# An attention and mixture-layer kernel: products with V, row shifts, warm-up and weight conversion placed elsewhere in the slots

## The chip, the cores and the metric

The kernel runs on one core of a Trainium2 chip. The metric is device time in microseconds (us), from the launch to the end of one execution. The core has TensorE (PE: matrix products, written to PSUM), VectorE (DVE), ScalarE (ACT), GpSimd (POOL) and DMA queues, of which SyncE (SP) starts most. PSUM has eight banks; a tile of `[128, 2, 512]` float32 takes two of them. PE, DVE, ACT and POOL each run their own list of instructions in order and wait for each other by semaphores.

## The reference, cut to what matters

```
q_rot, k_rot = rotate(q), rotate(k)             # rotary positions; 4 batches, 8 heads, 576 positions, 64 wide
scores = (q_rot @ k_rot.T) / 8
attn = exp(scores - max(scores)); attn = attn / (sum(attn) + 1e-9)
x = (attn @ v), heads side by side              # 2304 x 512
h = x @ w_in                                    # 2304 x 2048
out = (max(h, 0) + log1p(exp(-abs(h)))) @ w_out # 2304 x 512
```

All of it is float32. The kernel keeps that precision by splitting an operand into a high and a low part (`float32r`) and adding three products: high by high, low by high, high by low.

## The kernel before

**Attention in slots.** The 32 heads are taken as 16 pairs; the two heads of a pair lie on partitions 0 to 63 and 64 to 127, so that matmuls come in twos that run side by side ("a pair of matmuls" below), each over 288 columns. A pair of heads has ten slots. The loop at line 565 runs over slots s from 0 to 171; r is s modulo 10 and p is s divided by 10. Three stages are interleaved on PE in each slot:

- `p1(s)` (line 394) computes scores with queries on the partitions, three pairs of matmuls into a PSUM tile called s1, of which there is only one. VectorE reduces it to the negated row maximum (`mx`, line 408). After slots with r = 5 and r = 9, `shift0` (line 417) gathers the maxima of five or ten blocks (`sf`); one slot later `shift1` splits them on GpSimd into a high and a low part (`sh`).
- `shift2` (line 429) transposes these shifts on PE, with six matmuls of 64 columns for the first three blocks of a pair of heads and four for the last two; `shift3` (line 438) copies them from PSUM to `sm` on ScalarE. Before, both stand inside `p1` at r = 7 and r = 1: the transposes go into the free columns of the s1 tile behind the scores, ahead of the reduction in the code, and the copy stands behind it.
- `p2(n2)` with n2 = s - 9 (line 443), the score pass, computes the scores again with keys on the partitions: three pairs of matmuls, and a fourth that adds the shift. It goes to one of two PSUM tiles called s2. `exps` (line 455) exponentiates twice on ScalarE (first to `ph`, the high part, then in place), and `low` (line 462) subtracts on VectorE to give the low part `pl`. A tile s2 is free for the score pass two slots later when `low` has read it.
- `pv_mm(n3, part)` with n3 = s - 12 (line 471) multiplies with V. Five slots make one window, and c3 is n3 modulo 5, so c3 = 0 at r = 2 and 7, and c3 = 4 at r = 1 and 6. A window has 27 pairs of matmuls. In the kernel before, the slots with c3 = 0 to 3 do six of them (three in each of two parts) and the one with c3 = 4 does three. `evac` copies the result out on ScalarE at c3 = 4.

Within a slot PE's order is: part 0 of `pv_mm`, `p2`, part 1 of `pv_mm`, `p1`. Where c3 = 0 it is `p2`, part 0, `p1`, part 1; where c3 = 4 there is no part 1. All is held in the order of the code by `pin`.

**Keys.** The last block of 64 keys is stored twice (`pad`, line 337), so that the weights of the fifth block are 128 columns. ScalarE does this for the first two pairs of heads, GpSimd for the others, two small instructions a pair.

**Weight conversion beside it.** The weights arrive as 64-bit words. For six half-blocks `conv_w(..., spread=True)` (line 104) is advanced once in each slot of the table `PLAN` (line 44): a ScalarE step, a second one, four steps of two VectorE instructions each (`bits` and `sign`, lines 136 and 140), a GpSimd addition, a ScalarE rounding, a GpSimd subtraction. The VectorE steps use free columns of the s2 tile that `low` has just read, so that tile comes free only after them. `LOADS` names the slots in which their DMAs start on SP.

**Rows of x.** From slot 146 on GpSimd also prepares x for the next stage (`split`). GpSimd computes the rotary positions of later pairs throughout.

**Mixture layer.** From line 704 on, `emit_h` and `emit_o` run 96 units of TensorE work. Other conversions stand in it. The change doesn't touch it.

**Ahead of slot 0**, 108 matmuls on zeros (line 311) keep PE occupied while the first loads arrive. In slots 0 to 8 only `p1` runs.

Of the kernel before, what the change touches and what calls it, by code (L numbers as in the profile page):

```python
# [21 lines left out]
SP = 640  # L22
# [21 lines left out]
PLAN = tuple(tuple(b + i for i in (0, 5, 6, 10, 11, 15, 16, 20, 21)) for b in (59, 69, 84, 99, 114, 129))  # L44
LOADS = {33: (0, 0), 38: (0, 1), 43: (0, 2), 48: (0, 3), 53: (1, 0), 58: (1, 1), 63: (1, 2), 68: (1, 3), 73: (2, 0),
         78: (2, 1), 83: (2, 2), 88: (2, 3), 93: (3, 0), 98: (3, 1), 133: (3, 2), 138: (3, 3), 148: (4, 0), 153: (4, 1)}
# [7 lines left out]
def rope_attention_softplus_moe(  # L54
# [231 lines left out]
    def attention(es, es_r, es_s, tail):  # L286
# [3 lines left out]
        hl_p = pool(es, "hl", 3, "right")  # L290
        rp1 = pool(es_r, "rp1", 1, "right")
# [41 lines left out]
        def new_hl(p, i):  # L333
            hl_t[p, i] = hl_p.tile([128, 2, (S, SP)[i]], F32R, tag=f"hl{i}", name=f"hl{i}")
            return hl_t[p, i]

        def pad(t, j, e):
            rnd(t[:, j, S:], t[:, j, 512:S].bitcast(F32), e)

        def rope_steps(p, e="P"):  # L340
            for i in (1, 0):
                r, t = raw_t[p, i], new_hl(p, i)
                a, b = r[:, 1], r[:, 0]
                yield tt(a, a, tab[:, 0, :], ALU.mult, "P")
                yield tt(b, b, tab[:, 1, :], ALU.mult, "P")
                yield tt(a, a, b, ALU.add, "P")
                rnd(t[:, 0, :S], a, e)
                if i:
                    pad(t, 0, e)
                yield  # L350
                tt(t[:, 1, :S], a, t[:, 0, :S].bitcast(F32), ALU.subtract, "P")
                if i:
                    pad(t, 1, e)
                yield
# [4 lines left out]
        def rope_first():  # L359
# [16 lines left out]
            for j in range(2):  # L376
                pad(hl_t[0, 1], j, "A")
# [16 lines left out]
        def p1(n):  # L394
# [12 lines left out]
            x = shift2(s_g[r](p), sp) if r in s_g and s_g[r](p)[0] >= 0 else None  # L407
            pin(nc.vector.tensor_reduce(out=mx[p % 2][:m, j, c, :], in_=sp[:m, :, :HS], axis=AX.X, op=ALU.max,  # L408
                                        negate=True))
            if x is not None:  # L410
                shift3(s_g[r](p), x)
# [15 lines left out]
        s_g = {7: lambda p: (p, 0), 1: lambda p: (p - 1, 1)}  # L427

        def shift2(pg, t):
            p, g = pg  # L430
# [7 lines left out]
        def shift3(pg, x):  # L438
            p, g = pg
            pin(nc.scalar.copy(out=sm[p % 2][:, cut(g), :].rearrange("p c (t x) -> p t c x", t=2),  # L440
                               in_=x.rearrange("p t (c x) -> p t c x", x=64)))

        def p2(n):
            p, r = divmod(n, 10)
            j, c = divmod(r, 5)
            q, k = hl_t[p, 0], hl_t[p, 1]
            ck, cq = slice(c * 128, c * 128 + 128), slice(j * HS, (j + 1) * HS)
            sp = ps2[n] = ps_2.tile([128, 2, 512], F32, tag="s2", name="sp2")
            bias = sm[p % 2].rearrange("p c x -> p (c x)")
            for t, (a, b) in enumerate((*terms, (2, 2))):  # L450
                for i, o in enumerate(rows):
                    lhs, rhs = (k[o, b, ck], q[o, a, cq]) if t < 3 else (ones[o, :], bias[o, cq])
                    pin(nc.tensor.matmul(out=sp[:, i, :HS], lhsT=lhs, rhs=rhs, start=(t == 0), stop=(t == 3)))  # L453

        def exps(n):
            sp = ps2[n][:, :, :HS]
            ph = p_p.tile([128, 2, HS], F32R, tag="ph", name="ph")
            pin(nc.scalar.activation(out=ph, in_=sp, func=AF.Exp, scale=D ** -0.5))  # L458
            pin(nc.scalar.activation(out=sp, in_=sp, func=AF.Exp, scale=D ** -0.5))  # L459
# [9 lines left out]
        side = {}  # L469

        def pv_mm(n, part):
            p, r = divmod(n, 10)
            j, c = divmod(r, 5)
            flip = (c + part) % 2
            if c == 0 and part == 0:
                if n // 5 == NSLOT // 5 - 2:
                    pv_t[n // 5] = ps_1.tile([128, 2, 512], F32, tag="s1", name="pv")
                else:
                    pv_t[n // 5] = ps_v.tile([128, 2, 512], F32, tag="pv", name="pv")
            pv, vt = pv_t[n // 5], vs[p % 2]  # L480
            ph, pl = p_t[n]
            if side.get("flip", flip) != flip:
                hold = pin(nc.tensor.nop())
                for x in side["two"]:
                    tc.add_manual_dep(hold.ins, x.ins.name,
                                      mybir.DependencyInfo(mybir.DependencyClass.Sync, mybir.DependencyReason.DATA))
            two = []
            for t, (w, x) in enumerate(((0, ph), (2, ph), (0, pl))):
                for o in rows:
                    i = (o.start // 64 + flip) % 2  # L490
                    m = 64 if w else 128
                    lhs = vt[o, i, c, w:w + 1 + (w == 0), :].rearrange("p a d -> p (a d)")
                    ins = pin(nc.tensor.matmul(out=pv[:m, i, :HS], lhsT=lhs, rhs=x[o, i, :],  # L493
                                               start=(c == 0 and part == 0 and t == 0),
                                               stop=(t == 2 and c == 4)))
                    if t == 2:
                        two.append(ins)
            side.update(flip=flip, two=two)
            if part or c == 4:
                p_t.pop(n)  # L500
# [53 lines left out]
        nc.gpsimd.memset(ones.bitcast(F32), 1.0)  # L554
        for i in range(2):
# [9 lines left out]
        for s in range(NSLOT + LAG + PVD):  # L565
# [3 lines left out]
            c3 = n3 % 5  # L569
            if has3 and c3:  # L570
# [3 lines left out]
            if has2:  # L574
                p2(n2)
                exps(n2)
# [8 lines left out]
            if s == NSLOT + 1:  # L585
                last = (NP - 1, 1)
                shift3(last, shift2(last, ps_1.tile([128, 2, 512], F32, tag="s1", name="st")))
# [184 lines left out]
```

## Time and profile before

| | us |
|---|---|
| median of 3 runs | 737.51 |
| the three runs | 737.23 to 738.17 |
| the profiled execution | 738.13 |
| its span, first to last instruction | 736.3 |
| PE busy | 709.4 (96%) |
| DVE busy | 483.0 (66%) |
| ACT busy | 390.2 (53%) |
| POOL busy | 312.4 (42%) |

Busy time of PE is a union of records whose ends are modelled and overlap, so a busy PE need not be dense; the start times of consecutive matmuls tell the real pace. An idle time in square brackets is time that the engine stood still before the instruction, with the engine and line that let it go on. The attention takes about the first 328 us of the span, the mixture layer the rest.

### The profile page before, as it was taken

How to read it: one execution, taken by the hardware profiler on the slowest of the kernel's cores; microseconds unless marked ns; L12 is line 12 of the kernel's file. 1: busy time of each engine (PE TensorE's matmuls, PEld its weight loads, DVE VectorE, ACT ScalarE, POOL GpSimd, SP SyncE). 2: the span in 40 equal slices, each digit the busy share in tenths (PEclk: the TensorE clock that was granted, in tenths of full speed). 3: DMA queues.
4: the chain of work that ended last, by engine and by line, in shares of the span. 5: the costliest groups of instructions: out<-in, count | busy, mean ns of one | idle time of the engine just before them, and what ended most of it. 6: DMA issues, size and time to landing. Idle time of an engine off the chain costs nothing.

```text
span 736.3 us, 15495 instructions
## 1 busy us (share of the span) xinstructions
PE 709.4 (96%) x6255; PEld 651.9 (89%) x6255; DVE 483.0 (66%) x821; ACT 390.2 (53%) x706; POOL 312.4 (42%) x373
## 2 busy tenths in 40 slices
PE   8999999999999999989999999999999999999998
PEld 7899999888888889878899998999989989899896
DVE  6677778888888778757989987463454343444333
ACT  3677778778788777765665654222222232222222
POOL 5898888899898898680000000460400000000000
PEclk9899999999999999999999999999999999999999
DMA  7133444334433452103333422160010010001001
GB/s 273 71 101 115 127 130 130 122 89 124 125 102 123 117 153 67 33 18 95 115 114 116 136 94 65 43 204 12 23 44 1 0 44 1 0 1 44 1 0 44
DMA packets 30792, 59.23 MB, mean 80 GB/s; under 512 B 5056, under 2 KB 17664, under 8 KB 30720
## 3 DMA queue, kind: packets, MB, share of 16 engines
q1 hardware_dynamic: 27840, 53.06, 23.5%
q10 hardware_dynamic: 2880, 5.18, 1.9%
q8 instruction: 49, 0.80, 0.5%
q14 instruction: 23, 0.19, 0.1%
HBM read 48.64 MB, written 7.23 MB: 76 GB/s over the span
## 4 chain that ended last, share of the span: by engine, by line
PE 83%; DVE 10%; POOL 3%; ACT 2%; issue 1%; DMA 1%; SPq 0%; DVEq 0%; ACTq 0%; POOLq 0%
PE hp L214 27%; PE oa L253 14%; PE ob L253 14%; PE pv L493 12%; PE sp L453 9%; PE sp L405 7%; DVE mx L408 4%; DVE pl L466 3%; DVE sp L136 1%; DMA raw<-qk 1%; DVE wc L140 1%; POOL raw L331 1%; PE sp L434 1%; ACT sm L440 1%; DVE sf L418 0%
## 5 line engine op out<-in xcount | busy, mean ns | idle before, releaser
L214 PE MATMUL hp<-x,wh 128*128 128x384 f32 x768 | 196.5, 337 | 0.0
L226 ACT ACTIVATE e<-e 128x384 f32<-128x384 f32 x96 | 50.4, 525 | 203.8 <-DVE e L224 199.1
L408 DVE TENSOR_REDUCE mx<-sp 128x2 f32<-128x576 f32 (+1 forms) x160 | 120.5, 754 | 54.2 <-PE sp L405 43.7
L214 PEld LDWEIGHTS hp<-x,wh 128*128 128x128 f32 x768 | 140.7, 188 | 8.7 <-issue 0.5
L458 ACT ACTIVATE ph<-sp 128x576 fp32r<-128x576 f32 x160 | 104.4, 652 | 55.7 <-PE sp L453 55.1
L214 PE MATMUL hp<-x,wl 128*128 128x384 f32 x384 | 129.3, 337 | 0.0
L493 PE MATMUL pv<-ph,vs 64*128 64x288 f32 (+1 forms) x1152 | 126.2, 294 | 1.1 <-ACT sm L440 0.8
L466 DVE TENSOR_TENSOR pl<-sp,ph 128x576 fp32r<-128x576 f32 x160 | 119.8, 749 | 10.4 <-ACT sp L459 7.4
L453 PE MATMUL sp<-hl,hl 64*128 64x288 f32 x960 | 96.9, 304 | 15.0 <-DVE wc L140 10.9
L224 DVE TENSOR_SCALAR e<-hp 128x384 int32<-128x384 int32 x96 | 53.4, 556 | 80.3 <-PE hp L214 80.3
L459 ACT ACTIVATE sp<-sp 128x576 f32<-128x576 f32 x160 | 103.7, 648 | 0.0
L405 PE MATMUL sp<-hl,hl 64*128 64x288 f32 (+1 forms) x960 | 97.5, 306 | 3.6 <-DVE mx L408 1.8
L253 PE MATMUL oa<-wh,g 128*128 128x512 f32 x288 | 97.7, 393 | 0.0
L253 PE MATMUL ob<-wh,g 128*128 128x512 f32 x290 | 97.4, 391 | 0.0
L453 PEld LDWEIGHTS sp<-hl,hl 64*128 64x128 f32 x960 | 73.5, 187 | 22.7 <-DVE wc L140 16.0
L493 PE MATMUL pv<-pl,vs 64*128 64x288 f32 x576 | 87.8, 292 | 0.0
L331 POOL TENSOR_TENSOR raw<-raw,tab 128x576 f32<-128x576 f32 x60 | 84.6, 1432 | 6.4 <-DMA raw<-qk 6.4
L234 DVE TENSOR_TENSOR g<-m,g 128x384 fp32r<-128x384 f32 x96 | 56.0, 584 | 47.0 <-ACT g L231 47.0
L405 PEld LDWEIGHTS sp<-hl,hl 64*128 64x128 f32 (+1 forms) x960 | 71.7, 176 | 12.6 <-DVE mx L408 6.3
L229 DVE SCALAR_TENSOR_TENSOR m<-hp,e 128x384 f32<-128x384 f32 x96 | 53.5, 557 | 43.5 <-ACT e L226 42.1
L493 PEld LDWEIGHTS pv<-ph,vs 64*128 64x128 f32 (+1 forms) x1152 | 79.2, 158 | 2.7 <-PE pv L493 1.2
L231 ACT CAST g<-m 128x384 fp32r<-128x384 f32 x96 | 49.3, 513 | 48.6 <-DVE m L229 45.8
(91 smaller groups left out, 986.3 us busy)
## 6 DMA issues: line engine op xcount, KB each, us to landing
raw<-qk SPq DMA_DIRECT2D x30, 576.0 KB
wraw<-w SPq DMA_DIRECT2D x23, 512.0 KB
vf<-v SPq DMA_DIRECT2D x16, 320.0 KB
wraw<-w SPq DMA_DIRECT2D x14, 256.0 KB
x<-xt SPq DMA_DIRECT2D x32, 72.0 KB
xd<-xt SPq DMA_DIRECT2D x32, 72.0 KB
x<-rd SPq DMA_DIRECT2D x16, 144.0 KB
out<-wc ACTq DMA_DIRECT2D x9, 256.0 KB
```

The costliest lines, as they stand in the source:

```text
L214: pin(nc.tensor.matmul(out=hp, lhsT=a[f][:, c * 128:(c + 1) * 128], rhs=piece(j, c)[:, b, :], start=(i == 0), stop=(i == 11),))
L229: pin(nc.vector.scalar_tensor_tensor(out=m, in0=hp, scalar=0.0, in1=e, op0=ALU.max, op1=ALU.add))
L234: pin(nc.vector.tensor_tensor(out=g[:, 1, :], in0=m, in1=g[:, 0, :].bitcast(F32), op=ALU.subtract))
L253: pin(nc.tensor.matmul(out=po[:, z], lhsT=g[:, s, t * 128:(t + 1) * 128], rhs=b[f][:, 512 + z.start:512 + z.stop], start=(first and i == 0 ...
L331: pin((nc.vector if e == "V" else nc.gpsimd).tensor_tensor(out=out, in0=in0, in1=in1, op=op))
L405: pin(nc.tensor.matmul(out=sp[:m, i, :HS], lhsT=q[o, a, c * 128:c * 128 + m], rhs=k[o, b, j * HS:(j + 1) * HS], start=(t == 0), stop=(t == ...
L408: pin(nc.vector.tensor_reduce(out=mx[p % 2][:m, j, c, :], in_=sp[:m, :, :HS], axis=AX.X, op=ALU.max, negate=True))
L453: pin(nc.tensor.matmul(out=sp[:, i, :HS], lhsT=lhs, rhs=rhs, start=(t == 0), stop=(t == 3)))
L458: pin(nc.scalar.activation(out=ph, in_=sp, func=AF.Exp, scale=D ** -0.5))
L459: pin(nc.scalar.activation(out=sp, in_=sp, func=AF.Exp, scale=D ** -0.5))
L466: pin(nc.vector.tensor_tensor(out=pl, in0=sp[:, :, :HS], in1=ph.bitcast(F32), op=ALU.subtract))
L493: ins = pin(nc.tensor.matmul(out=pv[:m, i, :HS], lhsT=lhs, rhs=x[o, i, :], start=(c == 0 and part == 0 and t == 0), stop=(t == 2 and c == 4)))
```

## The change

Seven edits, all in the attention:

1. A window's 27 pairs with V are dealt out as 5, 6, 5, 6, 5 (`turns` and `cuts`): 3 and 2, then 4 and 2, 4 and 1, 5 and 1, 5 and 0 in the two parts of the slots.
2. The transposes of the shifts leave `p1`. They stand ahead of `p2` at r = 2 and r = 8, in the free columns of that slot's s2 tile. The copy to `sm` stands between the two exponentials of that slot.
3. The first transposes, for slot 9, get an s2 tile of their own after `p1(7)`.
4. The last ones lose their own s1 tile and go the same way as the others.
5. In slots 0 to 8 four more matmuls over 288 columns follow `p1`, into an s2 tile that nobody reads.
6. Keys lie in three fixed tiles `kk`, without copies of the last block; the fifth block's weights are read at another offset for each head of the pair (`key`).
7. `PLAN` starts at slot 23, 43, 63, 83, 103 and 123. `LOADS` begin at slot 13.

```
-PLAN = tuple(tuple(b + i for i in (0, 5, 6, 10, 11, 15, 16, 20, 21)) for b in (59, 69, 84, 99, 114, 129))
-LOADS = {33: (0, 0), 38: (0, 1), 43: (0, 2), 48: (0, 3), 53: (1, 0), 58: (1, 1), 63: (1, 2), 68: (1, 3), 73: (2, 0),
-         78: (2, 1), 83: (2, 2), 88: (2, 3), 93: (3, 0), 98: (3, 1), 133: (3, 2), 138: (3, 3), 148: (4, 0), 153: (4, 1)}
+PLAN = tuple(tuple(20 + 20 * n + i for i in (3, 9, 10, 14, 20, 24, 25, 29, 30)) for n in range(6))
+LOADS = {13 + 5 * (i % 2) + 20 * (i // 2): divmod(i, 4) for i in range(12)} | {
+    103: (3, 0), 108: (3, 1), 133: (3, 2), 141: (3, 3), 148: (4, 0), 153: (4, 1)}
...
+        kk = [at1.tile([128, 2 * S + 64], F32R, name=f"kk{i}") for i in range(3)]
...
-                if i:
-                    pad(t, 0, e)
...
-            x = shift2(s_g[r](p), sp) if r in s_g and s_g[r](p)[0] >= 0 else None
             pin(nc.vector.tensor_reduce(out=mx[p % 2][:m, j, c, :], in_=sp[:m, :, :HS], axis=AX.X, op=ALU.max,
                                         negate=True))
-            if x is not None:
-                shift3(s_g[r](p), x)
...
-        s_g = {7: lambda p: (p, 0), 1: lambda p: (p - 1, 1)}
...
+        def key(p, i, b, c):
+            x = b * S + (c * 128 if c < 4 else 512 if i else 448)
+            return kk[p % 3][rows[i], x:x + 128]
...
-        def exps(n):
+        def exps(n, between=None):
             sp = ps2[n][:, :, :HS]
             ph = p_p.tile([128, 2, HS], F32R, tag="ph", name="ph")
             pin(nc.scalar.activation(out=ph, in_=sp, func=AF.Exp, scale=D ** -0.5))
+            if between:
+                between()
             pin(nc.scalar.activation(out=sp, in_=sp, func=AF.Exp, scale=D ** -0.5))
...
+        turns = [(c, f, t) for c, ff in enumerate(((1, 0), (0, 1), (1, 0), (0, 1), (1,))) for f in ff for t in range(3)]
+        cuts = ((0, 3, 5), (5, 9, 11), (11, 15, 16), (16, 21, 22), (22, 27, 27))
...
+            for c, flip, t in turns[cuts[c3][part]:cuts[c3][part + 1]]:
...
+            g = {2: (p - 1, 1), 8: (p, 0)}.get(r)
...
+                x = shift2(*g, ps2[n2]) if g else None
                 p2(n2)
-                exps(n2)
+                exps(n2, (lambda: shift3(*g, x)) if g else None)
...
-            if s == NSLOT + 1:
-                last = (NP - 1, 1)
-                shift3(last, shift2(last, ps_1.tile([128, 2, 512], F32, tag="s1", name="st")))
+            if s == 0:
+                wp = ps_2.tile([128, 2, 512], F32, tag="s2", name="wp")
+            if s < LAG:
+                for i, o in enumerate(2 * rows):
+                    pin(nc.tensor.matmul(out=wp[:, i % 2, :HS], lhsT=ones[o, :], rhs=hl_t[0, 0][o, 0, :HS], start=True,
+                                         stop=True))
+            if s == 7:
+                shift3(0, 0, shift2(0, 0, ps_2.tile([128, 2, 512], F32, tag="s2", name="st")))
```

On PE, around slots 21 and 22 (r = 1 and 2), the list of the kernel before reads as follows; `sp` with `hl,hl` at L405 is `p1`, at L453 `p2`, `sh` and `identr` are the transposes, and `pv` the products with V:

```order
L453 MATMUL sp_827<-hl_323,hl_299 128x288 x6
L453 MATMUL sp_827<-sm_119,ones 128x288 x2
L405 MATMUL sp_839<-hl_414,hl_581 128x288 x6
L434 MATMUL sp_839<-identr,sh_117 128x64 x4
L453 MATMUL sp_856<-hl_323,hl_299 128x288 x6
L453 MATMUL sp_856<-sm_119,ones 128x288 x2
L493 MATMUL pv<-ph,vs_126 128x288 x2
L493 MATMUL pv<-ph,vs_126 64x288 x2
L493 MATMUL pv<-pl,vs_126 128x288 x2
L405 MATMUL sp_875<-hl_414,hl_581 128x288 x6
```

And in the changed kernel (L399 is `p1`, L446 `p2`, L422 the transposes, L489 the products with V):

```order
L446 MATMUL sp_864<-hl,kk_100 128x288 x6
L446 MATMUL sp_864<-sm_122,ones 128x288 x2
L399 MATMUL sp_876<-kk_101,hl 128x288 x6
L422 MATMUL sp_887<-identr,sh_120 128x64 x4
L446 MATMUL sp_887<-hl,kk_100 128x288 x6
L446 MATMUL sp_887<-sm_122,ones 128x288 x2
L489 MATMUL pv<-ph,vs_129 128x288 x2
L489 MATMUL pv<-ph,vs_129 64x288 x2
L489 MATMUL pv<-pl,vs_129 128x288 x2
L399 MATMUL sp_911<-kk_101,hl 128x288 x6
```

The transposes stand at the same place in the row, but now write the tile of the score pass behind them, no longer that of `p1` ahead of them.

On ACT, in the same slots before (L458 and L459 are the two exponentials, L440 the copy of the shifts):

```order
L458 ACTIVATE ph<-sp_827 128x576
L459 ACTIVATE sp_827<-sp_827 128x2x288
L440 CAST sm_119<-sp_839 128x2x2x64
L458 ACTIVATE ph<-sp_856 128x576
L459 ACTIVATE sp_856<-sp_856 128x2x288
```

And in the changed kernel (L451, L454 and L427):

```order
L451 ACTIVATE ph<-sp_864 128x576
L454 ACTIVATE sp_864<-sp_864 128x2x288
L451 ACTIVATE ph<-sp_887 128x576
L427 CAST sm_122<-sp_887 128x2x2x64
L454 ACTIVATE sp_887<-sp_887 128x2x288
```

The copy moved behind the first exponential of the next slot, and reads that slot's own tile.

On PE, slots 5 to 9 of the changed kernel (in the one before, the rows of L590 are missing and the transposes stand ahead of `sp_416`'s row in the tile of the row before):

```order
L399 MATMUL sp_363<-kk_99,hl 128x288 x6
L590 MATMUL wp<-hl,ones 128x288 x4
L399 MATMUL sp_377<-kk_99,hl 128x288 x6
L590 MATMUL wp<-hl,ones 128x288 x4
L399 MATMUL sp_394<-kk_99,hl 128x288 x6
L590 MATMUL wp<-hl,ones 128x288 x4
L422 MATMUL st<-identr,sh_119 128x64 x6
L399 MATMUL sp_416<-kk_99,hl 64x288 x6
L590 MATMUL wp<-hl,ones 128x288 x4
L446 MATMUL sp_429<-hl,kk_99 128x288 x6
```

Four matmuls were added behind each `p1`, and the six transposes have a tile `st` of their own.

## Rows read from the trace of the kernel before

**Rows 1.** Busy time by stretch: length, busy us per engine, PEclk, DMA share, GB/s
```profile
21.00:28.00 7.00, 6.54 (x50) 5.90 (x52) 4.41 (x8) 4.63 (x9) 6.84 (x8) 0.51 0.37 129
...
113.00:310.00 197.00, 183.49 (x2598) 173.21 (x2596) 159.02 (x272) 152.89 (x270) 168.48 (x194) 1.00 0.37 110
...
330.00:730.00 400.00, 399.94 (x2017) 361.37 (x2016) 227.96 (x405) 145.93 (x277) 34.45 (x41) 1.00 0.17 53
```

**Rows 2.** Timeline of PE: score passes of slots 9, 13, 28, 38, 159; start, length
```profile
20.36 0.56 PE L453 MATMUL sp<-hl,hl 64*128 64x288 f32 x6
...
29.65 0.57 PE L453 MATMUL sp<-hl,hl 64*128 64x288 f32 x6
...
57.42 0.57 PE L453 MATMUL sp<-hl,hl 64*128 64x288 f32 x6
...
75.85 0.57 PE L453 MATMUL sp<-hl,hl 64*128 64x288 f32 x6
...
310.54 0.55 PE L453 MATMUL sp<-hl,hl 64*128 64x288 f32 x6
```

**Rows 3.** Timeline, slots 33, 35 and 36: start, length, engine, line, what [idle before]
```profile
67.09 0.42 PE L493 MATMUL pv<-ph,vs 64*128 64x288 f32 x4
...
67.35 0.65 ACT L458 ACTIVATE ph<-sp 128x576 fp32r<-128x576 f32 x1 [1.03 <-PE sp L453]
67.49 0.56 PE L405 MATMUL sp<-hl,hl 64*128 64x288 f32 x6
...
67.90 0.65 ACT L459 ACTIVATE sp<-sp 128x576 f32<-128x576 f32 x1
...
68.09 0.76 DVE L408 TENSOR_REDUCE mx<-sp 128x2 f32<-128x576 f32 x1 [0.70 <-PE sp L405]
...
68.77 0.75 DVE L466 TENSOR_TENSOR pl<-sp,ph 128x576 fp32r<-128x576 f32 x1
...
69.99 0.59 PE L453 MATMUL sp<-hl,hl 64*128 64x288 f32 x6
...
71.55 0.76 DVE L408 TENSOR_REDUCE mx<-sp 128x2 f32<-128x576 f32 x1 [0.31 <-PE sp L405]
...
72.37 0.66 PE L405 MATMUL sp<-hl,hl 64*128 64x288 f32 x6
72.42 0.17 DVE L418 TENSOR_REDUCE sf<-mx 128x6 f32<-128x12 f32 x1
72.50 0.75 DVE L466 TENSOR_TENSOR pl<-sp,ph 128x576 fp32r<-128x576 f32 x1
...
73.31 0.40 PE L453 MATMUL sp<-hl,hl 64*128 64x288 f32 x2 [0.28 <-DVE pl L466]
```

**Rows 4.** Timeline, slots 31 and 32: transposes, score pass, copy of the shifts, next `p1`
```profile
63.71 0.30 PE L434 MATMUL sp<-identr,sh 64*128 64x64 f32 x4
63.87 0.67 PE L453 MATMUL sp<-hl,hl 64*128 64x288 f32 x6
...
64.85 0.37 ACT L440 CAST sm<-sp 128x256 fp32r<-128x256 f32 x1 [0.28 <-DVE mx L408]
...
65.28 0.40 PE L405 MATMUL sp<-hl,hl 64*128 64x288 f32 x2 [0.21 <-ACT sm L440]
```

**Rows 5.** Timeline, slots 90 to 92: second exponential, low part, next use of the tile
```profile
176.72 0.65 ACT L459 ACTIVATE sp<-sp 128x576 f32<-128x576 f32 x1
...
177.41 0.76 DVE L466 TENSOR_TENSOR pl<-sp,ph 128x576 fp32r<-128x576 f32 x1 [0.19 <-ACT sp L459]
...
178.87 0.67 PE L453 MATMUL sp<-hl,hl 64*128 64x288 f32 x6 [0.79 <-DVE wc L140]
```

**Rows 6.** Timeline of PE, slots 7 to 9: first transposes, first shift term of a score pass
```profile
19.58 0.52 PE L434 MATMUL sp<-identr,sh 64*128 64x64 f32 x6 [0.98 <-POOL sh L331]
...
21.46 0.61 PE L453 MATMUL sp<-sm,ones 64*128 64x288 f32 x2 [0.55 <-ACT sm L440]
```

**Rows 7.** Timeline of PE, slot 162: the next to last window's first product with V
```profile
316.69 0.53 PE L493 MATMUL pv<-ph,vs 64*128 64x288 f32 x4 [0.80 <-ACT sm L440]
```

## What the change will do to the time

> **What bounds the kernel now.** I read the busy time by stretch first. In the mixture layer PE is busy 399.94 of 400 us; in the attention 183.49 of 197, with POOL at 168.48, DVE at 159.02, ACT at 152.89 [rows 1]. So only the attention has time to give, and there PE is the fullest engine, but not full. Next the starts of PE's groups. A pair of matmuls takes 0.133 us where nothing waits (67.09 to 67.49, three pairs) [rows 3]. A slot of 13 pairs should take 1.72, a window of 62 pairs 8.2, ten slots 16.43 plus the transposes. The transposes cost 0.16 for four (63.71 to 63.87) [rows 4]; six I estimate at 0.24. PE's floor for ten slots is 16.83. Measured are 18.43 without conversion (57.42 to 75.85) [rows 2]: 1.6 us of standing still. From slot 13 to slot 159 there are 146 slots in 280.89 us (29.65 to 310.54) [rows 2]; 14.6 times 18.43 is 269.1, so the 24 VectorE steps of the conversion, with all else that is irregular, cost 11.8, or 0.49 each. Then the clock: from 21 to 28 us the granted clock is 0.51, the lower level, 1.2 GHz; before it, PE had three pairs (0.40) for each reduction of 0.76 and a wait of 0.98 [rows 1, 3, 6]; after it, with dense work, the full 2.4 GHz.
>
> Where the 1.6 us lie is seen in the timeline. After a `p2` that ends at T, the first exponential starts at T + 0.26, the second 0.55 later, `pl` at the earliest 0.69 after that; `mx` starts 0.60 after `p1` starts, and `pl` 0.68 after `mx`, or 0.95 with `sf` between (71.55 to 72.50); PE may use the score tile again 0.81 after `pl` starts, and s1 0.82 after `mx` starts [rows 3, 5]. At r = 5 to 7 before: `p2(5)` at 0 (69.99), `p1` at 0.93, `mx` 1.53, `pl` 2.48, tile free 3.29. Since the slot with c3 = 4 holds only seven pairs, PE is there at 2.65 and waits 0.64. The row says 3.32 (73.31) [rows 3], so the rules hold. A wait also costs 0.10 behind it: a group of six lasts 0.66 to 0.67 after one, 0.56 to 0.57 without [rows 3, 4, 5]. At r = 2 `p1` waits because s1 is held until the copy of the shifts, itself behind `mx`, has read it: 65.28, where three pairs of PV after a score pass that starts at 63.87 would bring it to 64.80 [rows 4].
>
> **The change part by part.**
>
> PV dealt out, and the transposes moved. The number of pairs between two score passes doesn't change: 16, 13, 13, 13, 7 before and after. What changes is that `p1` follows `p2` after two pairs, one, one and none instead of three, so `mx` comes up to 0.27 earlier. I work the two tight places by the rules. r = 5 to 7: `p1` at 0.66, `mx` 1.26, `pl` at the later of 2.03 (exponentials) and 2.21 (`mx` and `sf`), tile free 3.02, PE there at 2.65: wait 0.37. `p1(6)` waited 0.10 for s1 before (2.35 against 2.25); now s1 is free at 2.08. r = 0 to 2: DVE is still in the `pl` of slot 9 and starts `mx` at 1.54; `p1(1)` waits 0.11; tile free at 3.03, PE there at 2.76: wait 0.27, and only then come the transposes. The s1 tile is no longer held by the copy, so the wait at r = 2, 0.48 with its restart, goes. At r = 8 the six transposes find their tile free 0.05 before they need it, because ScalarE is behind there with `evac`: no wait. Ten slots: 16.83 + 0.37 + 0.11 + 0.27 + 0.1 for sums of restarts and small waits = 17.7. The gain is 0.73 per ten slots, over 14.6 of them 10.7 us. Bounds: 0, if the waits only change place, and 1.6 times 14.6 = 23, if all go. I take 10.7, because the same rules gave 3.29 for a row of 3.32.
>
> The copy between the exponentials. It lasts 0.37 [rows 4] and makes `pl` that much later in two slots of ten. At r = 2 and r = 8, 25 and 22 pairs lie between the end of that score pass and the next use of its tile, 3.3 and 2.9 us, against 1.9 + 0.81 for the chain with the copy: covered by 0.2 at least. If the cover were gone it would be 0.37 in each of 30 slots, 11 us.
>
> The Trainium skill, in "PSUM — Partial Sum Buffer", section "Terms", says that two engines may not be in one PSUM bank at once, reads beside reads included. The trace agrees as far as it goes: the copy waited for `mx`, which only read the same tile [rows 4]. By that rule the transposes can't be laid into the tile while `low` still reads it; that is the sum above. Without it their 0.16 at r = 2 could hide in the wait, 2.3 us less in all.
>
> The conversion. The 24 steps are the same in number, now one at each r = 0 and r = 4 from slot 30 to 144. At r = 0 the tile is needed two slots later, where PE waits anyway, so the step is felt whole: 178.87 minus 177.41 is 1.46 against 0.81, so 0.65 each. At r = 4 the step delays `mx` and `pl` of slot 5; by the rules that ends as 0.38 at r = 7. Twelve of each are 12.4; five times two ScalarE steps fall in one slot just ahead of r = 0 and cost some 0.25 each, 1.3 more. So 13.7 against 11.8: a loss of 1.9 us. Bounds: a gain of 11.8 (all hidden) and a loss of 4 (24 times 0.65).
>
> The earlier `LOADS` move six DMAs ahead on SP to where the DMA share is 0.37 [rows 1]: no cost that I can see. Pads gone: some POOL and ACT time, on engines that aren't waited for here; nothing.
>
> The start. The first copy of shifts no longer waits for `mx(7)`, so the score pass of slot 9 loses its 0.55 [rows 6]. PE gets there at about 20.5: transposes 19.58 to 19.83, three and two pairs. Slots 9 to 11 hold seven pairs, 0.93 at full clock, and are then bound by DVE at 0.68 + 0.76 = 1.44; slot 12 has 16 pairs and four transposes, 2.3. So slot 13 begins at 27.2 instead of 29.65: 2.4 us gained if the clock stays at 2.4 GHz. With the four added matmuls PE has five pairs, 0.67, for every 0.76, so I think it does. The matmuls themselves lie in time in which PE waits for `mx`. If the clock falls all the same, the gain is 0.5 and may be followed by a slow spell in dense work.
>
> The end. The next to last window no longer waits for the last copy, since that tile is gone: 0.80 [rows 7] and its restart, and some 0.2 from the shorter parts: 1.1 us. POOL's rows of x come 10 us sooner in need; POOL has 28.5 us idle in 197 [rows 1], enough.
>
> The sum: 10.7 - 1.9 + 2.4 + 1.1 = 12.3. The profiled execution took 738.13; 725.8 by it, and 725.2 by the median of 737.51, which I round to **725 us**.
>
> **The rivals.**
>
> (a) The clock falls all the same. For it: 0.51 over seven us [rows 1], and the wait of 0.98 for POOL's shifts stays [rows 6]. Against: PE then is more than four fifths busy in the slots before. It takes away 2.4 and up to 7 us at half rate would cost another 1 to 3: 728 to 730.
>
> (b) The waits only change place: `mx` earlier, but `pl` bound by ScalarE, whose exponentials do not move. For it: 2.03 is only 0.18 below 2.21. The 10.7 shrinks to about 2, and the time is 734.
>
> (c) Slower: the copy between the exponentials. At r = 2 and 8 it delays the second exponential, then the first of the next slot, `pl`, and, as DVE goes in order, the next `mx`. If each of 30 copies costs PE its 0.37 twice plus a restart, 0.84, that is 25 us, less 12.3: 750. It decides from 0.41 per copy on. Against it stand the covers worked out above.
>
> (d) Better: the conversion's steps hide where VectorE has more room, as the balanced slots leave it. With half of 13.7 hidden, 718; with a good part of the remaining waits too, 713.
>
> (e) The new clock or load edits do nothing and the rest is as forecast: that is (a) again, 727.
>
> **How the numbers follow.** My forecast (721 to 729) has 0.60; (a) with (e) 0.16; (b) 0.07; (c) 0.05; (d) 0.12. For 8 in 10 the range goes from 716 to 732: it leaves out (b), (c) and half of (d), 0.18. About 0.2%, 1.5 us, is what a measurement of this kernel can tell from no change. Only (c) ends on its slow side, 0.05; between (b) and (c) I leave 0.03 for an outcome inside it; the rest is faster, 0.92.
>
> **What would show it.** Right: no `p1` waits for ScalarE's copy; ten slots without conversion take 17.6 to 17.8; the wait at r = 7 is about 0.4; a score pass at r = 2 waits for the conversion by about 0.9; the granted clock is 1.00 from 21 to 28 us; slot 13 begins near 27; no wait for ScalarE in the next to last window. Wrong: waits of PE for ScalarE's second exponential or of the transposes for GpSimd; a clock of 0.5 anywhere in the attention; ten slots of 18 or more without conversion, or of 17.5 or less with it.

## The result, and the profile after

| us | before | after |
|---|---|---|
| median | 737.37 (737.17 to 738.17) | 730.31 (730.17 to 730.60) |
| the profiled execution | 738.13 | 730.17 |
| its span | 736.3 | 728.2 |
| score pass of slot 13 starts | 29.65 | 29.81 |
| ... of slot 159 | 310.54 | 303.48 |
| first matmul of the mixture layer | 328.42 | 320.12 |

Four runs each, on one chip: the ratio is 0.9903, with a 95% interval of 0.9886 to 0.9920. The kernel is 7.1 us faster, where 12.3 were forecast; 730.3 lies inside the range of 716 to 732, and outside the narrower 721 to 729 to which the prediction gave 0.60. The span shows where the 8.1 us of the profiled execution lie: the start lost 0.16, slots 13 to 159 gained 7.22 (280.89 to 273.67), and what follows slot 159 gained 1.04 (425.76 to 424.72).

Busy time of the changed kernel by stretch (columns as in [rows 1]; the attention ends about 8 us sooner, so the last two stretches are moved up):

```profile
21.00:28.00 7.00, 5.42 (x56) 4.77 (x56) 4.75 (x8) 4.07 (x7) 6.84 (x8) 0.81 0.39 133
...
113.00:303.00 190.00, 179.27 (x2608) 173.24 (x2607) 156.37 (x261) 149.28 (x264) 162.99 (x175) 1.00 0.39 114
...
322.00:722.00 400.00, 399.94 (x2019) 361.40 (x2018) 228.20 (x405) 146.00 (x277) 35.62 (x41) 1.00 0.17 53
```

The mixture layer is as before. The granted clock of 21 to 28 us is 0.81, no longer 0.51, but not 1.00 as forecast: the fall to 1.2 GHz now comes later (before, the granted clock was 0.76 from 20 to 22 us; after, 1.00 from 22 to 24 and 0.84 from 24 to 26). PE's score passes of slots 9, 13, 19, 29 and 159, which answer [rows 2]:

```profile
20.73 0.67 PE L446 MATMUL sp<-hl,kk 64*128 64x288 f32 x6
...
29.81 0.58 PE L446 MATMUL sp<-hl,kk 64*128 64x288 f32 x6
...
40.55 0.56 PE L446 MATMUL sp<-hl,kk 64*128 64x288 f32 x6
...
58.36 0.56 PE L446 MATMUL sp<-hl,kk 64*128 64x288 f32 x6
...
303.48 0.56 PE L446 MATMUL sp<-hl,kk 64*128 64x288 f32 x6
```

Slots 19 to 28, the only ten slots between the start and slot 149 without a VectorE step of the conversion ("without conversion" below), take 58.36 - 40.55 = 17.81; before, the tens from slots 19, 29, 39 and 49 took 18.42 to 18.46. From slot 29 on the tens with conversion take 18.7, every second one from slot 49 on 19.15; before, they took 19.05 with one step and 19.5 to 20.1 with more.

In those ten slots PE's timeline has the row behind the wait at r = 7 that answers [rows 3], and the transposes ahead of the score pass at r = 2 that answer [rows 4], with `p1` behind:

```profile
44.58 0.60 PE L399 MATMUL sp<-kk,hl 64*128 64x288 f32 x6
45.19 0.41 PE L422 MATMUL sp<-identr,sh 64*128 64x64 f32 x4
45.41 0.67 PE L446 MATMUL sp<-hl,kk 64*128 64x288 f32 x6
...
46.42 0.58 PE L399 MATMUL sp<-kk,hl 64*128 64x288 f32 x6
...
52.75 0.58 PE L446 MATMUL sp<-hl,kk 64*128 64x288 f32 x6
...
54.07 0.68 PE L446 MATMUL sp<-hl,kk 64*128 64x288 f32 x6 [0.20 <-DVE pl L461]
```

No `p1` waits for ScalarE's copy any more. The score pass of slot 27 still waits for `pl`; from the score pass of slot 26 to it there are 1.32 us for seven pairs (0.93), so 0.39 are lost.

### The profile page after: what moved, and what is told of

It reads as the page before. It is cut to its first block, busy times and chain, and to the rows that moved or that the text cites. A ratio compares the mean times of both kernels' runs of the same rounds, so it can differ in the third digit from the quotient of the medians.

```text
span 728.2 us, 15479 instructions
## 1 busy us (share of the span) xinstructions
PE 702.8 (97%) x6291; PEld 651.3 (89%) x6291; DVE 483.4 (66%) x821; ACT 388.7 (53%) x702; POOL 307.6 (42%) x348
## 4 chain that ended last, share of the span: by engine, by line
PE 76%; DVE 10%; POOL 9%; ACT 2%; issue 2%; DMA 1%; SPq 0%; DVEq 0%; POOLq 0%; ACTq 0%
PE hp L213 28%; PE oa L252 14%; PE ob L252 14%; PE pv L489 8%; PE sp L446 7%; DVE pl L461 4%; PE sp L399 4%; DVE mx L401 4%; POOL raw L331 3%; PE sp L422 1%; ACT sp L454 1%; DMA raw<-qk 1%; POOL vs L331 1%; POOL wl L160 1%; POOL hl L331 1%
## 5 line engine op out<-in xcount | busy, mean ns | idle before, releaser
L451 ACT ACTIVATE ph<-sp 128x576 fp32r<-128x576 f32 x160 | 104.4, 652 | 62.8 <-PE sp L446 62.5
L489 PE MATMUL pv<-ph,vs 64*128 64x288 f32 (+1 forms) x1152 | 134.0, 292 | 0.2
L461 DVE TENSOR_TENSOR pl<-sp,ph 128x576 fp32r<-128x576 f32 x160 | 120.4, 753 | 20.1 <-ACT sp L454 18.8
L454 ACT ACTIVATE sp<-sp 128x576 f32<-128x576 f32 x160 | 103.2, 645 | 1.0
L446 PE MATMUL sp<-hl,kk 64*128 64x288 f32 x960 | 98.0, 305 | 4.9 <-DVE pl L461 4.9
L399 PE MATMUL sp<-kk,hl 64*128 64x288 f32 (+1 forms) x960 | 95.6, 299 | 3.4 <-DVE mx L401 1.1
L489 PE MATMUL pv<-pl,vs 64*128 64x288 f32 x576 | 89.3, 292 | 0.0
L489 PEld LDWEIGHTS pv<-ph,vs 64*128 64x128 f32 (+1 forms) x1152 | 85.6, 158 | 1.7 <-PE pv L489 1.2
L446 PEld LDWEIGHTS sp<-hl,kk 64*128 64x128 f32 x960 | 73.2, 186 | 9.8 <-DVE pl L461 8.4
L399 PEld LDWEIGHTS sp<-kk,hl 64*128 64x128 f32 (+1 forms) x960 | 72.5, 175 | 6.7 <-DVE mx L401 2.0
```

What stands on the lines that cost most here:

```text
L399: pin(nc.tensor.matmul(out=sp[:m, i, :HS], lhsT=q[o, a, c * 128:c * 128 + m], rhs=k[o, b, j * HS:(j + 1) * HS], start=(t == 0), stop=(t == ...
L461: pin(nc.vector.tensor_tensor(out=pl, in0=sp[:, :, :HS], in1=ph.bitcast(F32), op=ALU.subtract))
L489: two.append(pin(nc.tensor.matmul(out=pv[:m, i, :HS], lhsT=lhs, rhs=x[o, i, :], start=(c == 0 and flip == 1 and t == 0), stop=(t == 2 and ...
```

## The experiments

Where a part of the time is told, it is worked out from the starts of the score passes in each run's trace. "A ten" is the time from slot 19 to 29, 29 to 39 and so on. The edits are against the changed kernel.

### Added matmuls only in slot 0

```
-            if s < LAG:
+            if s < 1:
```

> The changed kernel with the four added matmuls only in slot 0, not in slots 1 to 8. Theory one (GpSimd's list sets slots 9 to 12, the added matmuls hide nothing else): 730 to 731 us, against 730.31 with them; slot 13's score pass near 29.8 us. Rival (the added matmuls shorten the spell at 1.2 GHz): the granted clock from 21 to 28 us falls from 0.81 to about 0.5 and the time goes to 731.5 to 733.

Measured: 730.22, runs at 728.95 and 731.49, twice each; ratio 0.9894 (0.9874 to 0.9915). In the profiled execution (731.49) PE's clock fell for longer:

```profile
21.00:28.00 7.00, 5.06 (x50) 4.38 (x48) 4.84 (x8) 4.06 (x7) 6.84 (x8) 0.78 0.38 128
28.00:35.00 7.00, 7.00 (x83) 7.00 (x82) 3.73 (x7) 3.94 (x7) 5.53 (x5) 0.73 0.02 5
```

Slot 13 starts at 30.65 and slot 19 at 41.91, 1.36 later than in the changed kernel; from there on both are alike. So the clock can fall with the added matmuls and without them. That they shorten the fall is suggested by these two traces, one of each kernel, and not shown.

### Values of the first pair later

```
-                if r in (5, 6, 7):
+                if r in (5, 6, 7) if p else s in (5, 8, 9):
```

> The changed kernel with GpSimd's two subtractions for the values of the first pair of heads in slots 8 and 9 instead of 6 and 7, so that the low part of the second pair's queries comes 1.7 us sooner. Theory one (GpSimd's list sets slots 9 to 12): the wait of 0.78 at slot 10's first-pass matmuls goes, slot 13's score pass starts at 28.0 to 28.8 instead of 29.81 and the time is 728.6 to 729.6. Rival (VectorE and the clock set these slots): same time within 0.5, 730.3.

Measured: 730.86 (729.33 to 732.22); ratio 0.9908 (0.9886 to 0.9931). The edit was made because of two waits of `p1` in slot 10 of the changed kernel (the third row is `p1` of slot 11):

```profile
22.86 0.40 PE L399 MATMUL sp<-kk,hl 64*128 64x288 f32 x2 [0.40 <-ACT sp L454]
24.04 0.54 PE L399 MATMUL sp<-kk,hl 64*128 64x288 f32 x4 [0.78 <-POOL hl L331]
...
25.50 1.09 PE L399 MATMUL sp<-kk,hl 64*128 64x288 f32 x6 [0.40 <-DVE mx L401]
```

The second and third pair of matmuls of this `p1` need the low part of the second pair's queries, `hl`, which GpSimd finishes at 23.98 because it splits V of the first pair of heads ahead of it:

```profile
21.75 0.88 POOL L331 TENSOR_TENSOR vs<-vf,vs 128x320 fp32r<-128x320 f32 x1
22.58 1.40 POOL L331 TENSOR_TENSOR hl<-raw,hl 128x576 fp32r<-128x576 f32 x1
```

With the edit that wait is gone, but another stands two slots on, behind the splitting of V and the shifts (GpSimd, then PE):

```profile
25.22 0.86 POOL L331 TENSOR_TENSOR vs<-vf,vs 128x320 fp32r<-128x320 f32 x1
26.05 0.20 POOL L328 TENSOR_SCALAR sh<-sf 128x4 fp32r<-128x4 f32 x1
26.34 0.21 POOL L331 TENSOR_TENSOR sh<-sf,sh 128x4 fp32r<-128x4 f32 x1
...
26.60 0.41 PE L422 MATMUL sp<-identr,sh 64*128 64x64 f32 x4 [1.36 <-POOL sh L331]
```

Slot 13 starts at 29.04 in this execution (729.53, granted clock 1.00 from 21 to 28 us), above the forecast of 28.0 to 28.8, and nothing is gained: the work moved back stands ahead of the next thing that PE needs.

### GpSimd's list ahead of slot 12 in order

```
-         **{s: ((2, 1),) for s in range(9, 19)}}
+         **{s: ((2, 2 if s < 13 else 1),) for s in range(11, 19)}}
```

together with the edit before: the rope pieces of the third pair now begin behind the shifts.

> The changed kernel with two pieces of GpSimd's work moved behind what slots 10 and 12 wait for: the subtractions for the values go to slots 8 and 9, and the rotary work of the third pair of heads starts at slot 11 instead of 9. Theory (GpSimd's list sets slots 9 to 12): neither the first pass of slot 10 nor the transposes of slot 12 wait for GpSimd by more than 0.2, slot 13's score pass starts at 27.2 to 27.9, the time is 727.5 to 729. Rival (the clock or VectorE sets them): slot 13 at 28.4 or later.

Measured: 728.37 (728.29 to 728.74); ratio 0.9874 (0.9859 to 0.9889). No row of PE in slots 9 to 12 names GpSimd any more, the clock is 1.00 from 21 to 28 us, and slot 13 starts at 27.93, 1.88 earlier than in the execution of 730.17 and 0.70 earlier than in one of the changed kernel without the fall of the clock (28.63, below):

```profile
22.95 0.88 PE L399 MATMUL sp<-kk,hl 64*128 64x288 f32 x6 [0.42 <-ACT sp L454]
...
27.93 0.60 PE L446 MATMUL sp<-hl,kk 64*128 64x288 f32 x6
```

So it is shown that the order of GpSimd's list held up slots 10 to 12. A part of the gain is lost again: in the ten from slot 19 the transposes wait 0.24 for GpSimd's shifts, and that ten takes 18.03.

### The changed kernel again

No edit.

> The changed kernel itself, unedited, beside the two others. Theory (the stretch of half clock after the start comes in some executions and not in others, and costs 1.4 to 2.8 us in those with it): the times fall in two groups, near 728.9 and 730.3 to 731.7 us, and the profile of an execution without the stretch has slot 13 at 28.4 to 28.9 us. Rival (the changed kernel always has that stretch, since its start is fixed): all times at 730.2 to 730.6 us and slot 13 at 29.8 us, as measured first.

Measured: 730.48, of 729.00, 730.31, 730.66 and 730.72. The profile is of the execution of 729.00, and there the clock didn't fall, while GpSimd's wait stood as before:

```profile
24.01 0.53 PE L399 MATMUL sp<-kk,hl 64*128 64x288 f32 x4 [0.78 <-POOL hl L331]
...
28.63 0.59 PE L446 MATMUL sp<-hl,kk 64*128 64x288 f32 x6
```

Slot 13 starts 1.18 earlier than in the execution of 730.17. So the fall costs 1.2 us in a part of the executions of one and the same program. What the added matmuls are worth stays open. Without them the times were 728.95 and 731.49, against 729.00 and 730.17 to 730.72 here; but the mean granted clock of the two executions of 728.95 is 0.997, that of the execution of 729.00 is 1.000, so the former may hold a fall that cost nothing, and no trace of them shows where.

### Products with V dealt out as before

```
-        cuts = ((0, 3, 5), (5, 9, 11), (11, 15, 16), (16, 21, 22), (22, 27, 27))
+        cuts = ((0, 3, 6), (6, 9, 12), (12, 15, 18), (18, 21, 24), (24, 27, 27))
```

> The changed kernel with one edit undone: a window's pairs with V are 6, 6, 6, 6, 3 again, three to a part. By the prediction's rules the wait at r = 7 grows back from 0.37 to 0.64, and the first pass of r = 6 waits 0.1 again: ten slots 0.3 to 0.5 longer, the time 734 to 737. Rival (dealing out gains nothing by itself, the transposes do it all): 730 to 731.

Measured: 734.50 (734.28 to 734.72); ratio 0.9956 (0.9942 to 0.9971). The ten without conversion takes 18.27, those with it 19.1 to 19.4; the wait at r = 7 is longer (interval 1.61, not 1.32; score passes of slots 26 and 27), and so is the interval from r = 1 to 2 (1.60, not 1.36). By the medians the dealing out is worth 4.2 us. But the clock didn't fall in this run (slot 13 at 28.65): slots 13 to 159 take 279.08 instead of 273.67, 5.4 us.

```profile
52.07 0.61 PE L446 MATMUL sp<-hl,kk 64*128 64x288 f32 x6
...
53.68 0.66 PE L446 MATMUL sp<-hl,kk 64*128 64x288 f32 x6 [0.28 <-DVE pl L461]
```

### Transposes back in the first pass

```
+            g = {7: (p, 0), 1: (p - 1, 1)}.get(r) if n > 7 else None
+            x = shift2(*g, sp) if g else None
...
+            if g:
+                shift3(*g, x)
...
-            g = {2: (p - 1, 1), 8: (p, 0)}.get(r)
+            g = (p - 1, 1) if s == NSLOT + 2 else None
```

The first lines stand in `p1`, around the reduction; the last transposes keep their new place.

> The changed kernel with one edit undone: from slot 11 on the transposes stand in the first-pass tile at r = 7 and 1 again, with the copy behind the maximum. By the prediction's rules the first pass at r = 2 waits for the copy, 0.3 to 0.5 in ten slots without a conversion step at r = 0, less where the score pass is held up by one anyway: 732 to 735. Rival (the copy between the exponentials costs as much as it saves): 729.5 to 731.

Measured: 729.29 (729.12 to 729.54); ratio 0.9886 (0.9869 to 0.9902). The ten without conversion takes 17.97, against 17.81; those with it 18.67 and 19.13, against 18.74 and 19.16. `p1` waits for ScalarE's copy again, as in [rows 4]:

```profile
45.53 0.66 PE L399 MATMUL sp<-kk,hl 64*128 64x288 f32 x6 [0.19 <-ACT sm L431]
```

but the score pass ahead of it starts 1.11 us after that of slot 21, not 1.36: the transposes into the s1 tile run in the time in which PE waits for the s2 tile, whereas in the changed kernel they need that tile themselves and start only with it. So the forecast of 732 to 735 was wrong. (The mean granted clock of these four runs is 1.000, so that the changed kernel's 729.00 is the time to compare with.) The move of the transposes is worth 0.16 in a ten without conversion and nothing in one with it; slots 13 to 159 take 273.74 in all, as in the changed kernel (273.67). With the dealing out undone, the same ten lost 0.46; the two add up to about the 0.61 to 0.65 that the change gains there.

### The table of the conversion as before

`PLAN` and `LOADS` are those of the kernel before; the rest is the changed kernel.

> The changed kernel with the tables of the conversion of the kernel before (its slots 65 to 144, loads from slot 33); all other edits stay. Theory one (a step costs by its place, c3 = 2 or 3, in both tables; spreading is worth nothing): 24 steps at 0.45 to 0.55 give 729 to 732. Rival (spreading is what gained): four steps in ten slots crowd VectorE, 0.8 a step, 736 to 739.

Measured: 731.50 (730.14 to 731.77); ratio 0.9908 (0.9893 to 0.9923). The tens from slot 19 to 58 take 17.8, those with conversion 18.4 to 20; slots 13 to 159 take 274.92, against 273.67. Spreading the same steps over more slots is worth about 1.2 us and no more: neither table puts them where they cost nothing.

### The conversion without VectorE's work

```
-                        bits(o, x)
-                        sign(o, x)
+                        if a == 0:
+                            pin(nc.vector.tensor_scalar(out=wf[:, :1], in0=wf[:, :1], ...))
```

> The changed kernel with the conversion's VectorE work left out: of its four pairs of operations per chunk one operation on a single column stays, so that the converted weights are wrong; ScalarE's and GpSimd's steps, the loads and the order stand. Theory: what the tens with conversion have over those without is the VectorE steps' at r = 2 and r = 7. Then the tens from slot 29 on fall from 18.74 and 19.16 us to 17.8 to 18.0, r = 1 to 2 goes back to 1.36 us and r = 7 to 1.31, and the time is 717.5 to 720 us. Rival: ScalarE's steps (0.68 and 0.64 us, twice at r = 9) or GpSimd's additions hold the score passes as well: the tens stay above 18.3 us, 724 us or more.

Measured: 717.52 (717.32 to 717.81), 13.0 us under the changed kernel's 730.48, some of it the clock, which didn't fall here (slots 13 to 159 take 262.10, 11.6 less); ratio 0.9726 (0.9710 to 0.9741). Seven of the twelve tens from slot 29 fall to 17.8, the other five only to 18.2. This settles which engine the score pass at r = 2 waits for. In the changed kernel (slots 31 and 32, whose score passes start 1.99 apart) the profile names GpSimd:

```profile
61.86 0.57 PE L446 MATMUL sp<-hl,kk 64*128 64x288 f32 x6
...
62.88 0.29 DVE L135 TENSOR_SCALAR sp<-wc 128x128 int32<-128x128 int32 x1
62.90 0.68 POOL L328 TENSOR_SCALAR kk<-raw 128x576 fp32r<-128x576 f32 x1
...
63.21 0.29 DVE L139 SCALAR_TENSOR_TENSOR wc<-wraw,sp 128x128 int32<-128x128 int32 x1
...
63.64 0.41 PE L422 MATMUL sp<-identr,sh 64*128 64x64 f32 x4 [0.67 <-POOL kk L328]
...
63.85 0.67 PE L446 MATMUL sp<-hl,kk 64*128 64x288 f32 x6
```

But the transposes need only `sh` from GpSimd, and that was done at 61.43; they start 0.14 after `sign` ends (63.21 + 0.29), and the wait leaves with VectorE's work. What stays in every second ten is ScalarE's: two steps of two chunks stand in one slot at r = 9, and the score pass at r = 2 then comes 0.42 late (ScalarE and PE of the run without VectorE's work, slots 70 to 72):

```profile
95.03 0.60 ACT L158 CAST wh<-wc 128x512 fp32r<-128x512 f32 x1
95.53 0.67 ACT L144 ACTIVATE wt<-wraw 128x512 int32<-128x512 uint32 x1
...
98.22 0.41 PE L422 MATMUL sp<-identr,sh 64*128 64x64 f32 x4 [0.42 <-DVE wc L150]
```

### Conversion's steps at other places of a window

```
-PLAN = ... for i in (3, 9, 10, 14, 20, 24, 25, 29, 30)) ...
+PLAN = ... for i in (3, 9, 12, 17, 22, 27, 28, 29, 30)) ...
```

VectorE's steps go from r = 0 and 4 to r = 2 and 7, ahead of the longest intervals.

> The changed kernel with the 24 VectorE steps of the conversion at r = 2 and 7 (c3 = 0) instead of r = 0 and 4; the same steps, the same slots to start. Theory one (the step costs because its tile is needed again after only 20 pairs of matmuls; behind the slots with c3 = 0 there are 29): ten slots fall from 18.74 and 19.16 to 17.8 to 18.1, the time to 718 to 721. Rival (VectorE is short of time as such, so the wait turns up at the next score pass or the next first-pass tile): ten slots stay at 18.5 or more, 728 to 730.

Measured: 725.40 (724.06 to 725.55); ratio 0.9825 (0.9811 to 0.9840). Neither range was met. Tens of 18.0, and 18.5 where two ScalarE steps meet at r = 9. But the ten from slot 149 takes 21.49, 3.1 more. The last chunk's ScalarE step waits for an addition that is late on GpSimd, and holds the exponentials behind it:

```profile
280.00 0.62 ACT L158 CAST wh<-wc 128x512 fp32r<-128x512 f32 x1 [2.17 <-POOL wc L155]
281.75 0.76 DVE L461 TENSOR_TENSOR pl<-sp,ph 128x576 fp32r<-128x576 f32 x1 [2.01 <-ACT sp L454]
...
282.65 0.41 PE L422 MATMUL sp<-identr,sh 64*128 64x64 f32 x4 [2.12 <-DVE pl L461]
```

Behind that wait PE's clock fell (columns as in [rows 1]):

```profile
280.00:283.00 3.00, 0.88 (x14) 0.67 (x13) 1.25 (x2) 3.00 (x6) 2.92 (x4) 1.00 0.00 0
283.00:286.00 3.00, 3.00 (x34) 3.00 (x34) 2.02 (x4) 1.91 (x4) 2.92 (x4) 0.64 0.47 113
286.00:289.00 3.00, 3.00 (x41) 3.00 (x39) 1.32 (x3) 1.19 (x2) 0.60 (x1) 0.79 0.09 30
```

The interval with the wait is 1.5 longer than in the changed kernel (3.45, not 1.93), and the two after it, in which PE works without a pause, 1.0 and 0.5 longer: about half of the 3.1 is the clock.

### Steps in roomy slots, 15 slots from chunk to chunk

```
-PLAN = ... 20 + 20 * n + i for i in (3, 9, 10, 14, 20, 24, 25, 29, 30)) ...
+PLAN = ... 20 + 15 * n + i for i in (3, 8, 12, 17, 22, 27, 28, 34, 35)) ...
```

`LOADS` follow at the same pace.

> The changed kernel with the conversion's VectorE steps at r = 2 and 7, its ScalarE steps at r = 3, 8, 4 and 9 with no two in one slot ahead of r = 0, a half-block every 15 slots, so that all is done by slot 130, before GpSimd prepares x. If the price of the conversion is the place of its steps: every ten slots 17.8 to 18.1, no alternate ten slots 0.5 longer, none of the 3.1 us lost at slot 151 when the steps stood at r = 2 and 7 but ended at slot 150; 718 to 720.5 us. Rival (GpSimd, with 16.5 us of work in 18, becomes the limit): transposes wait for its shifts, ten slots of 18.4 or more, 723 to 727.

Measured: 722.51 (721.09 to 722.56); ratio 0.9789 (0.9775 to 0.9804). The late place at slot 151 is gone (a ten of 17.95) and the tens are 18.0, but 18.4 to 18.9 where the steps of two chunks fell in one slot (slots 47, 62, 77, 92, 107), which the expectation did not count; the time is above its range. One step costs about 0.1 in such a slot, a second one there 0.4 to 0.9.

### Both repairs together

`PLAN` is `15 + 20 * n + i` for i in (3, 8, 12, 17, 22, 27, 28, 33, 34), `LOADS` five slots earlier, and GpSimd's list as above (its rope pieces are the third pair's; the expectation says second by a slip).

> Two edits of runs before this one together: GpSimd's list ahead of slot 12 put in order (values of the first pair in slots 5, 8 and 9, rope pieces of the second pair two in each of slots 11 and 12), and the conversion's steps in the slots with room, now 20 slots from chunk to chunk so that no two chunks' VectorE steps fall in one slot: first step at slot 18, VectorE steps at r = 7 and 2 alone. The theory (a conversion step costs what it sticks out over the room of its slot, and two in one slot stick out): every ten slots from slot 19 to slot 149 take 17.8 to 18.05 us, none 18.4 or more; slot 13 starts near 27.9 us with the clock at 1.00 from 21 to 28 us; slot 159 near 290 us; 715.5 to 718 us. First rival (VectorE is full, so that its steps cost their time wherever they stand): tens of 18.3 to 18.9 us with conversion, 721 to 725 us. Second rival (GpSimd is the bound of the head, and the conversion's loads and steps ten slots earlier delay it again): slot 13 at 28.6 us or later and the two edits do not add up, 719 us or more.

Measured: 719.01 (718.87 to 719.11); ratio 0.9747 (0.9733 to 0.9761). All tens up to slot 149 take 17.96 to 18.16, nearly the forecast, and slot 13 starts at 27.87, so both repairs add up. The ten from slot 149 takes 19.17 and keeps the time above the forecast. GpSimd works there on a step of the split of x ahead of the shifts for which PE waits:

```profile
277.23 1.45 POOL L195 TENSOR_TENSOR xm<-x 128x576 f32<-128x576 f32 x1
278.64 0.21 POOL L328 TENSOR_SCALAR sh<-sf 128x4 fp32r<-128x4 f32 x1
278.93 0.21 POOL L331 TENSOR_TENSOR sh<-sf,sh 128x4 fp32r<-128x4 f32 x1
...
279.19 0.41 PE L422 MATMUL sp<-identr,sh 64*128 64x64 f32 x4 [1.37 <-POOL sh L331]
```

### One step of the split behind the shifts

```
-SPLITS = {146: 2, 148: 0, 153: 0}
+SPLITS = {146: 2, 148: 0, 149: 0, 153: 0, 155: 1}
```

on top of the run above.

> The run with both repairs, and one step of the split of x (GpSimd, 1.45 us) moved from the tail of slot 149 to that of slot 155, so that the two GpSimd operations on the shift of the last pair but one stand ahead of it. Theory (the 1.2 us that the ten slots from slot 149 take over their neighbours there, 19.17 against 18.0, are GpSimd's list and nothing else): slot 151 comes 1.4 us after slot 150 instead of 2.72, the ten slots take 17.8 to 18.0, slot 159 starts near 291.1 us, and the time is 717.5 to 718.2 us. Rival (the wait goes to the next thing that is late there, the split then holds the start of the expert stage back): slot 151 recovers, but the span from slot 159 to the expert stage's first matmul grows over 16.65 us and the time stays at 718.8 us or more.

Measured: **717.61** (717.42 to 717.78); ratio 0.9729 (0.9716 to 0.9742), the fastest version here that does the whole work. The ten from slot 149 takes 17.82, PE's wait for the shifts is gone, and the span from slot 159 to the mixture layer doesn't grow (16.63):

```profile
276.96 0.19 POOL L328 TENSOR_SCALAR sh<-sf 128x4 fp32r<-128x4 f32 x1
277.24 0.21 POOL L331 TENSOR_TENSOR sh<-sf,sh 128x4 fp32r<-128x4 f32 x1
277.39 1.45 POOL L195 TENSOR_TENSOR xm<-x 128x576 f32<-128x576 f32 x1
...
277.54 0.41 PE L422 MATMUL sp<-identr,sh 64*128 64x64 f32 x4
```

The Trainium skill, in "PSUM — Partial Sum Buffer", section "Engine vs sequencer instructions", says that the queues of ScalarE, VectorE and GpSimd are strictly first in, first out. The two runs agree: 0.4 us of work that PE needs stood behind 1.45 that nobody needed yet, and changing only their order gave 1.35 us in that ten.

## Why the prediction was right, and where it was wrong

**Slots 13 to 159: right, the size somewhat under.** Forecast -10.7 and +1.9, measured -7.2. With 17.81 for a ten instead of 17.7, the first term is 0.62 times 14.6 = 9.05. What is left over the plain tens is 273.67 - 260.03 = 13.64, against 11.8 before: a loss of 1.8, as forecast (1.9). The two waits came as worked out: 0.39 at r = 7 (forecast 0.37), 0.27 in the interval from r = 1 to 2 (1.36 for seven pairs and four transposes, 1.09; forecast 0.27). The missing 0.11 are restarts: "0.1 for sums of restarts and small waits" was too little, the intervals show 0.06 at r = 0 and at r = 2, 0.12 at r = 7 to 8 and 0.08 at r = 8 over their pairs. They are 0.22 above that term; the wait of 0.11 for `p1(1)` stands in no row and takes half of it back.

**Which edit does it.** The prediction costed the dealing out and the move of the transposes as one term. Apart, they are 0.46 and 0.16 per ten without conversion, and with the conversion in place the move gives nothing: the wait at `p1`, 0.48, went, and 0.25 came back at the score pass ahead of it, whose tile the transposes now wait for. The prediction says that their 0.16 would hide in that wait if they need not wait for the tile; in the s1 tile, where they stood before, they do hide. For that one edit the rival that the waits only change place was mostly right, though not by its cause, ScalarE. (At c3 = 4 `p1` followed `p2` at once before too; "none instead of three" changes only c3 = 1 to 3.)

**The conversion: right.** Forecast 13.7; the twelve tens from slot 29 exceed twelve plain ones by 13.0 (226.74 - 213.72). Of that 11.2 leave with VectorE's work, 0.47 for each of 24 steps, and 1.9 stay, some 0.4 in each of five tens where two ScalarE steps meet (forecast 0.25). At r = 0 a step costs 0.63 (interval 1.99 for 1.36), at r = 4 it costs 0.29 (1.61 for 1.32), where 0.65 and 0.38 were worked out. The rule that a step is felt whole where PE waits anyway could have been turned round: the same steps at r = 2 and 7, behind which 16 pairs follow, cost 0.1 each. Rival (d) describes this, but the table of the change doesn't do it.

**The start: the step that failed.** Forecast -2.4, measured +0.16. The sentence "Slots 9 to 11 hold seven pairs, 0.93 at full clock, and are then bound by DVE" had left out GpSimd, though it is the fullest engine there, 6.84 of 7 us in [rows 1]. In the changed kernel it holds up slot 10 by 0.78, and putting its list in order takes that wait away. Of the 2.56 missing, 1.18 are the fall of the clock (29.81 against 28.63 in an execution without it), 0.7 are GpSimd's order (28.63 against 27.93), and 0.7 stand against the forecast of 27.2: slot 9 came 0.2 to 0.3 later than 20.5, and `p1` of slot 10 waits another 0.4, put down to ScalarE's exponential. "I think it does" of the clock was wrong too, and the bound given for this case, a gain of 0.5, was 0.7 too good. Rival (a), 728 to 730, comes within 0.3 of the time and names the clock, but not the rest of the cause: of GpSimd it has only the wait of 0.98 at the first transposes, and in no rival does GpSimd bound slots 10 to 12. That 730.3 lies inside the range says little of the start, which alone missed by 2.6; the range is 16 us wide.

**The end: right.** No wait for ScalarE in the next to last window any more, [rows 7]; from slot 159 to the first matmul of the mixture layer there are 16.64 us instead of 17.88, and 1.04 of it is left at the end of the span.

**The copy between the exponentials: covered, as said.** Rival (c) asked 0.84 for each of 30 copies; the ten without conversion shows no row of a wait for it. No run undoes the keys without pads, and the moved loads were undone only together with the table of the conversion, so that these cost nothing is not shown. The prediction has six DMAs moved ahead; by the two tables it is four, and nine come later.

In sum: the start is 2.6 short of the forecast, and the dealing out and the transposes 1.65; 12.3 less these 4.2 is the 8.1 that the span gained.

## What to carry to other kernels

Before a stretch is costed by the engines that wait in it, look at the one that is busy nearly all of it: a busy share of 0.98 off the path can be the next bound as soon as the path gets shorter, and its order can be worth more than its work. A step of side work costs what it sticks out over the room of its slot, so place it by the intervals that the trace shows, one to a slot: that brought the 13 us of conversion in the tens up to slot 148 down to about 3. Undo the parts of a change one at a time, since a wait that disappears from its row may stand one row later.

## What the runs showed of the hardware

PE's clock was not the same in each execution of one program: of the changed kernel's eight runs, seven took 730.2 to 730.7 and one 729.0, and the two profiles differ by a stretch of 1.2 GHz, granted clock 0.81 from 21 to 28 us in the one and 1.00 in the other. PE had the same waits ahead of it in both (0.40 and 0.78 in slot 10). The kernel before has such differences too: in the profiled execution of 738.13 the granted clock was 0.51 there, and its four runs lie between 737.17 and 738.17. Of the kernels above, six had times in two groups 1.2 to 2.9 us apart (with the changed kernel those without added matmuls, with later values, with the old table, and the first two with moved steps); the other six, three of them with the same waits at the start, lay within 0.5 us. What sets the fall off in one execution and not in another stays open. A single long wait had one behind it as well: after PE had stood still for 2.12 us near slot 152, the granted clock was 0.64 and 0.79 in the next two stretches of 3 us, and the dense work there took 1.5 us longer.

A releaser in the profile can be the wrong one where two engines end nearly together: for the transposes at r = 2 it named GpSimd's work on later keys, which ended at 63.58, VectorE's at 63.50, and the run without VectorE's work showed that it was VectorE.
